# Linear attention followed by a gelu MLP, one core: pair layout of k and v in two batches, x inside the first h tiles, v casts moved, q transposed by DMA

## The chip, the cores and the metric

The kernel runs on one core of one Trainium2 chip. The metric is device time in microseconds (us); lower is better. The kernel before takes 309.27 us (median of 3 runs, 308.99 to 309.62). A profile gives the "span", from the first to the last instruction, which lies 1.8 to 2.1 us under the time of the same run. Engines are named as in the profile: PE (TensorE matmul), DVE (VectorE), ACT (ScalarE), POOL (GpSimd), SP (SyncE, here the queue that issues nearly all DMA transfers).

## The reference, cut to what matters

Inputs: q, k, v of 8 batches x 8 heads x 576 rows x 64 columns; w_in 512 x 2048; w_out 2048 x 512; all float32.

```python
q_s = softmax(q, axis=-1)            # over the 64 columns
k_s = softmax(k, axis=2)             # over the 576 rows
kv  = einsum('bhsd,bhse->bhde', k_s, v)
x   = einsum('bhsd,bhde->bhse', q_s, kv)   # then heads side by side: 4608 x 512
h   = x @ w_in                       # 4608 x 2048
out = gelu_erf(h) @ w_out            # 4608 x 512
```

The 4608 rows go through in nine chunks of 512: rows 0 to 511 of each batch (chunks 0 to 7) and the last 64 rows of all batches together (chunk 8).

## The kernel before

Per chunk there is an h phase (16 tiles of 4 matmuls, each tile followed by a gelu on ACT) and a y phase (4 accumulators of 16 matmuls, each followed by an eviction on DVE and a store). The attention of a later batch is put between these matmuls by hand; every engine works its instructions off in program order. A pair is two of the eight heads (pairs 0 to 3); kv and x are made by pairs. w_in and w_out are loaded in parts, w_in in five (0 to 4), w_out in four (0 to 3). The parts of the code that matter here:

```python
def norm_q(b, parts=1, engs=None):        # e = exp(q)
    ...                                   # per part:
        nc.vector.reduce_sum(out=qsum[:, :, hs], in_=eq[:, :, hs, :], axis=AX.X)
        nc.vector.reciprocal(recq[:, :, hs], qsum[:, :, hs])
        engs[i % len(engs)].tensor_tensor(out=eq..., in0=eq..., in1=recq..., op=ALU.mult)

def tp_step(b, half, eng="v"):            # q to columns, on PE
    ps = psum_a.tile([128, J, 2, 128], BF16, tag="a")
    ...                                   # 8 x nc.tensor.transpose(ps, eq, identity)
    nc.vector.tensor_copy(out=o, in_=ps)  # or ACT

def dve_front(b):
    norm_q(b)                             # the product on GpSimd
    if b < B:
        cast_v_all(b)                     # 5 casts on VectorE

# ... loads of batch 0, w_in, w_out, batch 1, batch 2 ...
kv_chain(0, warm)                         # casts, kv, norm, x of batch 0, one after the other
h_phase(0, {...})
y_phase(0, {(2, 0): [norm_q(1)], (3, 3): [tp_step(1, 0)], (3, 7): [tp_step(1, 1, "s")]})
kv_chain(1)                               # the same for batch 1, after y phase 0
h_phase(1, {12: [cast_v_all(2)]})
y_phase(1, {(0, 15): [norm_q(2)], (1, 15): [kv_step(2, ...)], ...})
for c in range(2, B + 1):
    # h phase c: kv of batch c+1 after tiles 1, 2; tp_step after 4, 5; x after 8..11
    # y phase c: (1, 15): dve_front(c + 2)
```

(Lambdas and repeated arguments are cut.) A main load has runs of 1024 B and, for the last 64 rows, a second transfer with runs of 256 B.

The softmax here doesn't subtract the row's maximum and nothing guards it: scores larger than these inputs give would overflow.

## Time and profile before

| | before |
|---|---|
| time, us | 309.27 |
| span of the profiled run, us | 307.6 |
| PE busy | 288.6 us, 94% |
| mean granted clock of PE | 0.972 |
| DMA, mean rate | 151 GB/s |

How to read it: PE is busy nearly throughout, so the question for each part is whether it takes work out of PE's full stretch or closes one of its holes, all of which lie before 95 us. A phase of 64 undisturbed matmuls is 13.81 us. The lines are shown in the prediction.

### The profile page before, as it was taken

To read this page: it belongs to the slowest core of one execution; us is meant where nothing else is said; L and a number is where in the kernel's file an instruction comes from. 1 tells how busy PE (TensorE), PEld (TensorE's weight loads), DVE (VectorE), ACT (ScalarE), POOL (GpSimd) and SP (SyncE) were. 2 spreads that over 40 slices of the span, in tenths; PEclk is the share of its full clock that TensorE was granted. 3 is DMA by queue.
4 is the path that set the end of the run, shared out by engine and by line. 5 is a ranking of instruction groups with operands and counts; after the bars stand their busy time and mean duration, and the time that the engine had idled before them with its cause. 6 is when DMAs were issued, how large, how long until landed. Compare 5 with 4: busy or idle time off the path is not lost.

```text
span 307.6 us, 3824 instructions
## 1 busy us (share of the span) xinstructions
PE 288.6 (94%) x1541; PEld 138.4 (45%) x1541; DVE 122.0 (40%) x218; ACT 151.7 (49%) x212; POOL 38.3 (12%) x23
## 2 busy tenths in 40 slices
PE   5759998699899999999999999999999999999993
PEld 1424444244445544544454445444644455444441
DVE  4754437410777355342534344434433223110021
ACT  4546754367924582458245924591457056006400
POOL 6200002000204206000600060006000400000000
PEclk9588999699999999999999999999999999999999
DMA  7999999995026902691279117911600100110033
GB/s 219 316 381 387 369 263 304 312 304 152 2 102 190 286 23 84 188 271 51 73 207 270 37 69 213 265 36 68 153 21 34 70 34 0 36 70 33 2 68 68
DMA packets 47809, 46.38 MB, mean 151 GB/s; under 512 B 14000, under 2 KB 39600, under 8 KB 47792
## 3 DMA queue, kind: packets, MB, share of 16 engines
q1 hardware_dynamic: 47792, 46.14, 51.4%
q8 instruction: 12, 0.20, 0.3%
q14 instruction: 5, 0.04, 0.0%
HBM read 36.70 MB, written 9.44 MB: 150 GB/s over the span
## 4 chain that ended last, share of the span: by engine, by line
PE 89%; DVE 4%; ACT 3%; DMA 2%; issue 1%; POOL 1%; SPq 0%; ACTq 0%; DVEq 0%
PE ps L246 42%; PE ps L259 38%; PE ps L209 3%; PE ps L169 3%; PE ps L225 2%; DMA f<-in_q_dram 2%; ACT e L123 1%; DVE qsum L159 1%; PE ps L328 1%; DVE y_sb L266 1%; POOL e L161 1%; DVE xT L235 1%; PE ps L173 1%; DVE kvbd L197 0%; ACT L123 0%
## 5 line engine op out<-in xcount | busy, mean ns | idle before, releaser
L250 ACT ACTIVATE g<-ps 128x512 bf16<-128x512 f32 x144 | 86.0, 597 | 116.1 <-PE ps L246 116.1
L246 PE MATMUL ps<-xT,wi_bf 128*128 128x512 bf16 x576 | 136.5, 386 | 1.7 <-ACT wi_bf L294 1.7
L259 PE MATMUL ps<-wo_bf,g 128*128 128x512 bf16 x576 | 126.6, 379 | 1.2 <-DVE y_sb L266 1.2
L259 PEld LDWEIGHTS <-g 128*128 128x128 bf16 x576 | 56.3, 98 | 68.8 <-issue 1.9
L246 PEld LDWEIGHTS <-wi_bf 128*128 128x128 bf16 x576 | 55.9, 99 | 66.2 <-issue 4.7
L266 DVE COPY y_sb<-ps 128x512 f32<-128x512 f32 x36 | 24.8, 689 | 96.9 <-PE ps L259 96.9
L161 POOL TENSOR_TENSOR e<-e,recq 128x2048 bf16<-128x2048 bf16 (+1 forms) x9 | 33.9, 3765 | 203.8 <-DVE recq L160 171.4
L123 ACT ACTIVATE e<-f 128x2048 bf16<-128x2048 f32 (+1 forms) x20 | 31.2, 1563 | 7.9 <-DMA f<-in_q_dram 4.3
L235 DVE CAST xT<-ps 128x512 bf16<-128x512 f32 x32 | 21.8, 689 | 20.1 <-PE ps L225 16.8
L159 DVE TENSOR_REDUCE qsum<-e 128x16 f32<-128x1024 bf16 (+1 forms) x12 | 20.9, 1743 | 19.1 <-ACT e L123 18.9
L216 DVE COPY qT<-ps 128x1024 bf16<-128x1024 bf16 x17 | 11.6, 690 | 15.3 <-PE ps L209 15.3
L169 PE MATMUL ps<-v_aug,e 128*128 128x129 bf16 x128 | 11.7, 228 | 4.6 <-DVE v_aug L144 2.8
L209 PE MATMUL ps<-identity,e 128*128 128x128 bf16 x144 | 11.7, 229 | 4.0 <-POOL e L161 3.9
L169 PEld LDWEIGHTS <-e 128*128 128x128 bf16 x128 | 9.5, 101 | 9.9 <-DVE v_aug L144 2.6
L209 PEld LDWEIGHTS <-e 128*128 128x128 bf16 x144 | 9.9, 102 | 8.5 <-POOL e L161 5.0
L225 PE MATMUL ps<-qT,kvbd 128*128 128x512 bf16 x32 | 12.2, 401 | 1.5 <-ACT kvbd L193 1.2
L144 DVE CAST v_aug<-f 128x512 bf16<-128x512 f32 x32 | 11.7, 415 | 2.5 <-DMA f<-in_v_dram 2.5
L79 ACT ACT_TABLE_LOAD x9 | 11.5, 1283 | 0.9 <-PEq L439 0.7
L328 PE MATMUL ps<-zeros 128*128 128x512 bf16 x21 | 7.9, 528 | 1.2 <-DVE scr L69 1.2
L186 DVE RECIPROCAL rec<-ps 128x2 f32<-128x2 f32 (+1 forms) x18 | 3.0, 169 | 14.6 <-PE ps L173 14.6
L197 DVE TENSOR_TENSOR kvbd<-ps,rec 64x128 bf16<-64x128 f32 (+1 forms) x30 | 8.4, 278 | 0.9
L123 ACT ACT_TABLE_LOAD x6 | 7.7, 1283 | 0.1
(32 smaller groups left out, 63.1 us busy)
## 6 DMA issues: line engine op xcount, KB each, us to landing
out_dram<-y_sb SPq DMA_DIRECT2D x32, 256.0 KB, 2.3
f<-in_q_dram SPq DMA_DIRECT2D x6, 1024.0 KB, 7.5
f<-in_k_dram SPq DMA_DIRECT2D x6, 1024.0 KB, 10.5
f<-in_v_dram SPq DMA_DIRECT2D x6, 1024.0 KB, 10.2
w<-in_moe_w_out_dram SPq DMA_DIRECT2D x4, 1024.0 KB, 11.4
w<-in_moe_w_in_dram SPq DMA_DIRECT2D x3, 1024.0 KB, 11.1
f<-in_q_dram SPq DMA_DIRECT2D x4, 512.0 KB, 9.2
f<-in_k_dram SPq DMA_DIRECT2D x4, 512.0 KB, 8.9
```

The lines of the kernel that those rows point to most:

```text
L123: nc.scalar.activation(out=dst[:, i * n:(i + 1) * n], in_=src[:, i * n:(i + 1) * n], func=AF.Exp)
L144: nc.vector.tensor_copy(out=o[:, :, :, 0:D], in_=s[:, hp])
L159: nc.vector.reduce_sum(out=qsum[:, :, hs], in_=eq[:, :, hs, :], axis=AX.X)
L161: engs[i % len(engs)].tensor_tensor(out=eq[:, :, hs, :], in0=eq[:, :, hs, :], in1=recq[:, :, hs].unsqueeze(3).to_broadcast([128, J, n, D]) ...
L169: nc.tensor.matmul(ps, st[b]["ek"][:, j, hs, :].rearrange("p h d -> p (h d)"), v_aug[b % 2][:, j, hp, 0:PW], start=(j == 0), stop=False,)
L209: nc.tensor.transpose(ps[:, j, i, :], st[b]["eq"][:, j, 2 * hp:2 * hp + 2, :].rearrange("p h d -> p (h d)"), identity,)
L225: nc.tensor.matmul(ps, kvbd[b][:, hp, :], st[b]["qT"][:, :, hp, :], start=True, stop=True)
L235: nc.vector.tensor_copy(out=st[b]["xT"][:, hp, :], in_=ps)
L246: nc.tensor.matmul(ps, wi_bf[:, dm, t * 128:(t + 1) * 128], xT[:, dm, :], start=(dm == 0), stop=(dm == NDM - 1),)
L250: nc.scalar.activation(out=g[:, t, :], in_=ps, func=AF.Gelu)
L259: nc.tensor.matmul(ps, g[:, t, j * 128:(j + 1) * 128], wo_bf[:, t, :], start=(t == 0), stop=(t == NDF - 1),)
L266: nc.vector.tensor_copy(out=y_sb, in_=ps)
```

## The change

Its intent, in four parts. (1) k and v of batches 0 and 1 are loaded with 9 consecutive rows of one head on a partition: one run of 9 x 64 x 4 = 2304 B, one transfer where there were two; kv is then made by 9 matmuls per pair of heads. (2) x pairs 2 and 3 of batches 0 and 1 are made inside the first group of h tiles, and y phase 0 runs over four accumulators at once so that batch 1's attention lies between its matmuls. (3) q of batches 3 to 8 is transposed by DMA and not by PE. (4) The v casts of batches 4 to 7 no longer follow the norm of q. Besides: GpSimd casts some of v and w_in, 30 warming matmuls instead of 12, the last store in halves.

```diff
+    def load_pair(b, name, t, parts):
+        src = t[b].rearrange("h (p n) d -> (h p) (n d)", n=NS).rearrange("(x q) f -> q x f", q=128)
+        ...
+    def kv_pair(b, hp):
+        for n in range(NS):                       # NS = 9
+            nc.tensor.matmul(ps[:, 0:D + 1], ek_pair[...][:, hp % 2, n, :], v_pair[b][:, hp, n, 0:D + 1], ...)
+    def xbar_step(b):
+        nc.sync.dma_start_transpose(out=qT as (p, 16, 128), in_=eq as (p, 2048))
...
-    kv_chain(0, warm)
+    kv_pair(0, 0) ... norm_pair(0, 3, "s")
+    cast_wi(2, wi[2], "v")
+    h_phase(0, {...}, group=3, pre={1: [x_step(0, 2)], 2: [x_step(0, 3, "s")]})
...
-    y_phase(0, {...})
-    kv_chain(1)
+    for t in range(12):
+        for j in range(J): y_mm(0, yps[j], j, t)
+        if t == 9: tp_step(1, 0)
+    # then t = 12..15 of one accumulator after the other, with tp, kv and x of batch 1 between
...
     y_phase(1, {
-        (0, 15): [norm_q(2, parts=2)],
+        (0, 15): [norm_q(2, 0, 2)],
+        (1, 1): [norm_q(2, 1, 2, nc.vector)],
...
-    s[4 + d] = [lambda: tp_step(b, 0)]
-    s[5 + d] = [lambda: tp_step(b, 1)]
...
-            yi[(1, 15)] = [lambda nb=nb: dve_front(nb)]
+            yi[(1, 0)] = [lambda nb=nb: norm_q(nb)]
+            if nb == 4:
+                yi[(2, 0)] = [lambda: cast_v_all(4)]
+            elif nb < B:
+                yi[(0, 8)] = [lambda nb=nb: cast_v_all(nb)]
+            yi[(3, 0)] = [lambda nb=nb: xbar_step(nb)]
```

## The prediction

> **What bounds the kernel now.** I read the page of the profile first (engine shares, 40 slices), then the chain that ended last in order of time, then the timeline of the first 95 us, then the windows. The page says that TensorE (PE) carries the end:
>
> ```profile
> PE 288.6 (94%) x1541; PEld 138.4 (45%) x1541; DVE 122.0 (40%) x218; ACT 151.7 (49%) x212; POOL 38.3 (12%) x23
> PE   5759998699899999999999999999999999999993
> PEclk9588999699999999999999999999999999999999
> DMA  7999999995026902691279117911600100110033
> PE 89%; DVE 4%; ACT 3%; DMA 2%; issue 1%; POOL 1%; SPq 0%; ACTq 0%; DVEq 0%
> L209 PE MATMUL ps<-identity,e 128*128 128x128 bf16 x144 | 11.7, 229 | 4.0 <-POOL e L161 3.9
> ```
>
> PE is full from slice 8 on, at full clock; holes and half clock stand in slices 0 to 3 and 7, where the DMA engines are saturated. So time can come from two places only: the head (to about 95 us) and PE work taken out of the full stretch. The chain shows where (start us, us, what):
>
> ```profile
> 21.24 15.67 PE ps L246 x64
> 36.91 11.22 PE ps L259 x52
> ...
> 51.76 0.69 DVE y_sb L266
> ...
> 59.15 15.49 PE ps L246 x64
> ...
> 76.58 1.92 ACT e L123
> ...
> 102.07 0.45 PE ps L209 x8
> ...
> 103.38 0.45 PE ps L209 x8
> ...
> 275.20 13.81 PE ps L246 x64
> ...
> 302.87 0.69 DVE y_sb L266
> ```
>
> A dense 64-matmul phase costs 13.81 us (216 ns each) when nothing disturbs it. From this I made a ledger of the span: start to the first h matmul 21.2; 18 dense phases 18 x 13.81 = 248.7; h phases 0 and 1 over that, 15.67 - 13.81 = 1.9 and 15.49 - 13.81 = 1.7; transposes in y phase 0, 1.0; the hole between y phase 0 and h phase 1, 59.15 - 51.76 = 7.4; y phase 1 (74.5 to 93.1) over 13.81, 4.8; five batches 3 to 7 with 2.9 of attention on PE each (16.7 - 13.8 for the h phase in the windows), 14.5; batch 8, 1.8; tail after the last matmul 4.7. Sum 307.7, the span being 307.6. The time is 1.7 above the span (309.27 - 307.6).
>
> **What the Trainium skill says.** "TensorE: Matmul & The Clock Gate", Part 1 (What's actually happening): the array falls to half clock after an idle window of about 3.4 us and needs as long a busy one to come back. The trace agrees: after PE idled from 5.5 to 9.4 us the windows show a granted clock of 0.50 for 8 to 14 us, and again 0.50 at 22 to 24 and 56 to 62 us, where matmuls start 428 ns apart, not 216. "SBUF — State Buffer", Who interferes with whom: a VectorE cast in a two-port mode and a GpSimd instruction exclude one another. The trace agrees: GpSimd's 128x2048 product takes 4.91 us beside the v casts and 3.6 in batch 8, which has none. "GPSIMD Engine Reference", introduction: elementwise work runs about twice as fast on VectorE; no GpSimd cast is in this trace. "DMA: Bandwidth & Descriptors", Latency and other measured facts: a DMA transpose moves 261 GB/s where the middle dimension isn't contiguous, so 512 KB would be 2 us of transfer, an estimate; no run shows one yet.
>
> **Part 1: transposes by DMA, batches 3 to 8.** Removed from PE: 6 batches x 2 halves x 0.45 us (the chain's L209 x8 pieces) = 5.4 us, all on the path, since PE is full there. Removed from VectorE: 12 evictions of 0.69 us, hidden anyway. Added: six transposes in the sync queue. In a steady y phase starting at T, exp of q ends at T+3.7, the reduction runs after the first y eviction (T+4.4 to 6.7), GpSimd's product ends at about T+11, and the queue reaches the transpose after the third output, about T+11.3. It's needed by the first x matmul, after h tile 8, T+22.7. Slack 11 us, against a landing I estimate at 4 to 6 us (2 of transfer, 2.3 to landing as the small outputs show, some issue). Hidden. Batch 3 is tighter: both product halves end about 5.6 us into h phase 2, x comes after tile 12 (12.3 us): 6.7 us of slack. I allow 0.5 for it. The v casts move away from the product; that shortens it to 3.6, not on the path.
>
> **Part 2: batch 0.** k and v (2.36 MB) moved at a mean of 289 GB/s (window 6 to 13 us), with dips to 164 to 230 where the 256 B rests were in flight; weights with longer runs got 382 (24 to 37 us). At 375 it takes 6.3 us and not 8.2: everything behind comes 1.9 us earlier. The third w_in part, cast at 20.5 before, lands near 18.6. Exps of k cost more: four of 64x1152 at about 1.16 (scaled from 1.06 for 1024 columns) for 2.75 before; they end near 12.6. The kv pairs are 9 matmuls of 65 columns at about 57 ns (the 129-column ones start that far apart), 0.5 each. GpSimd casts three v quarters and four w_in halves; at an estimated 0.7 us each it ends at 16.8. So the first group of three h tiles can begin near 16, but in VectorE's order the eviction of x pair 2 stands behind the cast of w_in part 2: it comes near 20, and the group's last six matmuls after it. Six earlier ones (1.3 us) are already done: an effective start of 18.8, plus 0.4 for two x inside: 19.2 for 21.2. PE idles some 3 us before it, so I keep 1.7 for half clock.
>
> **Part 3: batch 1 inside y phase 0.** The phase runs t-outer over four accumulators up to t = 11, so transposes, kv and x sit between matmuls. The 7.4 us hole and the 1.7 at half clock go. In their place: transposes 0.9, four kv pairs 2.0, four x 0.9, and 0.5 of the last kv to x chain not covered: 4.3 for 1.0 + 7.4 + 1.7 = 10.1. The loads allow it: h phase 0 ends near 34, w_out part 3 lands near 37 and is cast by ScalarE about 40, needed at 45; k and v of batch 1 land near 41 and 44, kv starts at 47.
>
> **Part 4: y phase 1.** In the old order both reductions and the product of q stood ahead of the first y eviction, which came at 83.1, 6 us after its accumulator was done. Now only the first half stands ahead of it: eviction about 5.4 us into the phase, the buffer needed at 6.9. Left over: 2.9 of attention and about 0.7 waiting for exp of k: 3.6 for 4.8.
>
> **Part 5: the end.** The last eviction and store in halves on two queues: 4.2 for 4.7.
>
> **Sum.** 19.2 + 248.7 + 1.7 + 4.3 + 3.6 + 5 x 2.0 + 0.9 + 0.5 + 4.2 = 293.1 of span; plus 1.7 is 294.8. By part: head 2.2, batch 1 5.8, y phase 1 1.2, transposes 5.4 less 0.5, tail 0.5. I place the centre at 293.0, somewhat lower, since the 30 warming matmuls may save the half clock that I keep in h phase 0.
>
> **Rivals.** (a) The DMA transpose is slow, or holds up the sync queue. Nothing in the old trace measures it. Against it: 11 us of slack, and the 40-slice DMA row shows stretches of 0 to 2 tenths in each y phase. If landing took 15 us, x would wait about 4 us in each of six batches and in batch 3 more: 24 us back, a little above where it began at 310 to 320, the only way to slower. (b) The head stays bound by loads: the w_in parts set when h tiles can go (casts at 20.5, 23.2, 25.9 waited for the DMA), so reordering attention gives only 1.9 us, and in-order queues (GpSimd casts at twice my estimate, the eviction behind the cast) give that back: 297 to 299. (c) The gain of batch 1 is given back in y phase 1: it starts some 9 us earlier while batches 2 and 3 still load (the old trace's loads ended at 74 us). If they end about 70, exp of batch 3 has little margin; a late one delays h phase 2's gelus by 1 to 3 us. (d) PE stays warm throughout and the first group starts near 17: about 289.
>
> **Range and chances.** Parts 1 and 3 (some 11 us) rest on counted PE work and a visible hole; the head is uncertain by 3 each way. I predict 293.0, range 287.5 to 298.5. Faster by over 2% means under 303.1: it takes both rival (a) and another to miss it. Faster 0.95, within 2% 0.03, slower 0.02.
>
> **What would show it.** L209's successors: 48 PE transposes, not 144, and h phases of 15.8 us in batches 3 to 7, not 16.7, with no wait of x for the transpose; its landing under 10 us. First dense h stretch from about 20 and h phase 0 ending near 34. Full clock from 46 us on; h phase 1 beginning near 51 and ending near 66, not 74.5. The first y eviction of y phase 1 about 5.4 us in. Wrong would be: x waiting for the transpose each batch, half clock at h phase 1, loads of batch 3 ahead of an exp in the chain.

## The result, and the profile after

The changed kernel takes 294.3 us (median of 4 runs, 292.78 to 295.34) beside 309.36 for the kernel before (the three runs above and a fourth). The ratio is 0.951, 95% interval 0.9459 to 0.9562. Ratios here are the mean time of one kernel's fast runs over that of the other's of the same rounds, so not quite the ratio of the medians.

The page of the kernel after, the rows that answer to those shown of before (engines; PE, clock and DMA in 40 slices; the chain by engine):

```profile
PE 279.7 (96%) x1491; PEld 132.1 (45%) x1491; DVE 118.8 (41%) x211; ACT 154.8 (53%) x212; POOL 38.6 (13%) x34
PE   8849999999999999999999999999999999999993
PEclk9999999999999999999999999999999999999999
DMA  7999999999118946981698079816601600120033
PE 81%; DMA 9%; SPq 3%; DVE 2%; ACT 2%; issue 1%; ACTq 0%
```

PE has 9 us less of work and no hole after slice 2 that a tenth would show; the clock row is full in this run (although the first warming matmuls, until about 5 us, still start 0.43 us apart, not 0.216: the row doesn't show that cold start). The chain that ended last now goes through DMA for 9% of the span: 16.6 us in the head, which hangs on loads, and 10.0 us for the v of batch 5. In order of time (start us, us, what):

```profile
8.23 10.21 DMA w<-in_moe_w_in_dram
...
18.47 1.23 DVE wi_bf L403
19.70 0.61 DVE xT L318
...
20.35 1.04 PE ps L336 x4
...
33.44 8.63 PE ps L346 x40
...
97.58 13.81 PE ps L346 x64
...
132.30 0.44 DVE v_aug L210
...
134.12 0.61 DVE y_sb L365
...
134.77 7.07 PE ps L346 x32
```

(L336 are the h matmuls, L346 the y matmuls.) The first three lines are one story: a load of w_in, VectorE's cast of it, and only then the eviction of x that PE waits for until 20.35. The last three are another: a v cast, a y eviction behind it, and PE going on at 134.77. Cutting both chains at the same phase starts gives a ledger of the spans:

| stretch | before, us | after, us | less, us |
|---|---|---|---|
| start to y phase 0 | 36.91 | 33.44 | 3.47 |
| y phase 0, batch 1's attention, h phase 1 | 37.76 | 31.39 | 6.37 |
| y phase 1 | 18.49 | 16.94 | 1.55 |
| h and y phase 2 | 30.52 | 29.62 | 0.90 |
| h and y phase 3 | 30.52 | 30.45 | 0.07 |
| h and y phases 4 to 6 | 91.55 | 88.87 | 2.68 |
| h and y phase 7 | 29.45 | 28.56 | 0.89 |
| phase 8 and tail | 32.40 | 32.13 | 0.27 |
| sum | 307.60 | 291.40 | 16.20 |

Phases 2 to 7 would each give 0.9 by the DMA transposes; five of them do, and phase 3 gives nearly none. (In what was expected of the runs below, "batch 4" is this phase 3: batch 4's kv and x are made in it.) The trace by the tile that the transposes write, of the kernel after (issuing queue, instruction, count: ns min/median/max; then from issue to landing):

```profile
L289 SPq DMA_TRANSPOSE qT<-e x6: 1372/2078/2280, 87.4 to 228.5; - x6
DMA to landing us min/median/max: 4.3/4.4/4.9
```

The transpose issued at 111.41 landed 4.6 us later, near 116.0; x of that batch began after kv and nine tiles, at 120.1. No instruction waits for one.

The four runs of the changed kernel fall in two groups: 292.78 and 293.42 with a mean clock of 0.997 and 1.000, 295.18 and 295.34 with 0.991 and 0.988. Experiments e6 and e9 look into that.

### The profile page after: what moved, and what is told of

Same layout as the page of the kernel before. It is cut to its first block, busy times and chain, and to the rows that moved or that the text cites. A ratio compares the mean times of both kernels' runs of the same rounds, so it can differ in the third digit from the quotient of the medians.

```text
span 291.4 us, 3728 instructions
## 1 busy us (share of the span) xinstructions
PE 279.7 (96%) x1491; PEld 132.1 (45%) x1491; DVE 118.8 (41%) x211; ACT 154.8 (53%) x212; POOL 38.6 (13%) x34
## 4 chain that ended last, share of the span: by engine, by line
PE 81%; DMA 9%; SPq 3%; DVE 2%; ACT 2%; issue 1%; ACTq 0%
PE ps L346 38%; PE ps L336 38%; DMA w<-in_moe_w_in_dram 4%; DMA f<-in_v_dram 3%; DMA f<-in_k_dram 2%; SPq L121 2%; PE ps L237 2%; PE ps L305 2%; ACT ek L152 1%; PE ps L272 1%; DVE v_aug L210 1%; SPq L105 0%; DVE xT L318 0%; ACT L152 0%; PE ps L241 0%
## 5 line engine op out<-in xcount | busy, mean ns | idle before, releaser
L336 PE MATMUL ps<-xT,wi_bf 128*128 128x512 bf16 x576 | 132.3, 379 | 4.1 <-DVE xT L318 2.4
L346 PE MATMUL ps<-wo_bf,g 128*128 128x512 bf16 x576 | 127.9, 379 | 0.7 <-DVE y_sb L365 0.7
L336 PEld LDWEIGHTS <-wi_bf 128*128 128x128 bf16 x576 | 55.4, 98 | 69.3 <-issue 3.9
L346 PEld LDWEIGHTS <-g 128*128 128x128 bf16 x576 | 56.0, 98 | 67.0 <-issue 0.9
L229 POOL TENSOR_TENSOR e<-e,recq 128x1024 bf16<-128x1024 bf16 (+1 forms) x10 | 27.6, 2761 | 184.2 <-DVE recq L228 145.1
L152 ACT ACTIVATE e<-f 128x1024 bf16<-128x1024 f32 (+1 forms) x11 | 15.7, 1442 | 2.9 <-DMA f<-in_q_dram 2.8
L210 DVE CAST v_aug<-f 128x512 bf16<-128x512 f32 x24 | 10.3, 428 | 10.2 <-DMA f<-in_v_dram 9.5
L152 ACT ACTIVATE ek<-f 128x2048 bf16<-128x2048 f32 x6 | 11.4, 1898 | 0.0
L424 PE MATMUL ps<-kvbd 128*128 128x512 bf16 x35 | 9.7, 440 | 1.2 <-DVE scr L82 1.2
L202 DVE CAST vr_aug<-f 64x512 bf16<-64x512 f32 x6 | 5.6, 926 | 11.7 <-DMA f<-in_v_dram 11.7
L168 ACT ACTIVATE ek<-f 64x1152 bf16<-64x1152 f32 x8 | 9.3, 1162 | 1.3 <-DMA f<-in_k_dram 1.1
L237 PEld LDWEIGHTS <-ek 128*128 128x128 bf16 x96 | 6.8, 97 | 3.2 <-ACT ek L152 0.6
L237 PE MATMUL ps<-v_aug,ek 128*128 128x129 bf16 x96 | 8.1, 220 | 0.1
L259 DVE TENSOR_TENSOR kvbd<-ps,rec 64x128 bf16<-64x128 f32 x24 | 6.9, 289 | 0.6
```

The lines of the kernel that those rows point to most:

```text
L152: nc.scalar.activation(out=dst[:, i * n:(i + 1) * n], in_=src[:, i * n:(i + 1) * n], func=AF.Exp)
L210: nc.vector.tensor_copy(out=o[:, :, :, 0:D], in_=s[:, hp])
L229: eng.tensor_tensor(out=eq[:, :, hs, :], in0=eq[:, :, hs, :], in1=recq.unsqueeze(3).to_broadcast([128, J, w, D]), op=ALU.mult,)
L237: nc.tensor.matmul(ps, st[b]["ek"][:, j, hs, :].rearrange("p h d -> p (h d)"), v_aug[b % 2][:, j, hp, 0:PW], start=(j == 0), stop=False,)
L336: nc.tensor.matmul(ps, wi_bf[:, dm, t * 128:(t + 1) * 128], xT[:, dm, :], start=(dm == 0), stop=(dm == NDM - 1),)
L346: nc.tensor.matmul(ps, st[c]["g"][:, t, j * 128:(j + 1) * 128], wo_bf[:, t, :], start=(t == 0), stop=(t == NDF - 1),)
```

## The experiments

All are edits of the changed kernel, all gave correct results. Runs e1 to e4 shared one chip, e5, e6, e7 and e9 another, and e8, e10, e11 and e12 a third; medians and ratios are of their 4 to 6 runs, spans of the profiled one, to be read against 291.4. The changed kernel was not run again beside them, and its own runs spread over 2.6 us, so a difference of a few tenths between spans is read from the phases of the traces and not from the times.

**e1: the transposes back on PE.**

```diff
+        s[10 if late else 4] = [lambda: tp_step(b, 0)]
+        s[11 if late else 5] = [lambda: tp_step(b, 1)]
-        xbar_step(3)
-            yi[(3, 0)] = [lambda nb=nb: xbar_step(nb)]
```

> The changed kernel with the transposes of q of batches 3 to 8 put back on TensorE (h tiles 4 and 5, batch 3 at 10 and 11) and the DMA transposes gone. Theory (transposes on TensorE are pure added length where it is full, 0.90 us a batch): span 291.4 + 6 x 0.9 = 296.8, h phases of 16.7 us instead of 15.8. Part of the 0.85 us lost in batch 4 may come back, since the queue no longer carries the transposes: 296 to 297. Rival (the gain of batches 3 to 8 came from VectorE's or GpSimd's relief): no change from 291.4.

298.24 us, ratio 0.9651, span 296.2. Each pair of phases from 2 to 6 takes 30.52 us, 16.71 of it the h phase, as in the kernel before. Phase 3 loses only 0.07 by it, the five others 0.9 each; with 0.3 of a later start that is 4.9, and 4.8 was measured. So the DMA transposes are worth 0.9 us wherever PE is full. Phase 3's missing 0.8 is not a separate matter: the transpose stands in the one sync queue ahead of the loads of batch 5. That queue's timeline, of the kernel after first, then of e1:

```profile
111.41 2.27 SPq L289 DMA_TRANSPOSE qT<-e  x1
...
122.33 1.19 SPq L122 DMA_DIRECT2D f<-in_v_dram  x1
```

```profile
119.33 1.64 SPq L122 DMA_DIRECT2D f<-in_v_dram  x1
```

Counted from the start of h phase 3 (111.2 and 112.4), the v of batch 5 is issued at 11.1 us with the DMA transposes and at 6.9 without, and its casts begin at 21.1 and at 17.4 (20.0 to 20.7 in e4, e5, e6, e11 and e12, which keep the DMA transposes and these casts). In e1 PE waits for no y eviction, so the 0.8 comes back, as its expectation had allowed.

**e3: the v casts back behind the norm of q.**

```diff
             yi[(1, 0)] = [lambda nb=nb: norm_q(nb)]
-            if nb == 4: yi[(2, 0)] = [cast_v_all(4)]
-            elif nb < B: yi[(0, 8)] = [cast_v_all(nb)]
+            if nb < B: yi[(1, 0)].append(cast_v_all(nb))
```

> The changed kernel with the v casts of batches 4 to 7 put back right after the reduction of q, beside GpSimd's product. Theory (keeping them apart isn't worth anything by itself; it costs 0.7 us once, where the early cast of batch 5 waits for its v and holds up a y eviction): GpSimd's 128x2048 products 4.9 us instead of 3.6, span 0.5 to 0.9 us shorter, about 290.7. Rival (the casts kept apart are what lets the DMA transposes hide): x waits for the transposes, span longer by 1 us or more.

309.13 us, ratio 1.0008, span 307.9: the whole gain of the change is gone, and both expectations are wrong. x doesn't wait for a transpose, and the product isn't stretched to 4.9. VectorE's timeline in y phase 3 of this run (start us, us, engine, line, what):

```profile
138.08 0.35 DVE L228 RECIPROCAL recq<-qsum 128x32 f32<-128x32 f32 x1
138.35 0.36 DVE L202 CAST vr_aug<-f 64x512 bf16<-64x512 f32 x1
138.63 5.10 DVE L210 CAST v_aug<-f 128x512 bf16<-128x512 f32 x4
143.64 1.28 DVE L365 COPY y_sb<-ps 128x512 f32<-128x512 f32 x2
```

Four casts that take 0.43 each elsewhere take 5.10 together: the chain of this run shows one of them at 3.74, nearly the length of GpSimd's product, which ran from 138.56 for 3.95 us. The y eviction stands behind them, and PE's timeline of the same run has the price:

```profile
137.64 4.26 PE L346 MATMUL ps<-wo_bf,g 128*128 128x512 bf16 x18
144.37 5.30 PE L346 MATMUL ps<-wo_bf,g 128*128 128x512 bf16 x16 [2.47 <-DVE y_sb L365]
```

PE waits 2.47 us, and the 16 matmuls after it take 5.30 us; after the same wait in phase 2, of 2.71 us, they took 3.61. The windows show a granted clock of 0.61 and 0.53 from 144 to 148 us, and of 1.00 after the wait in phase 2. Against the changed kernel, phases 2 to 5 of this run are 2.9, 3.5, 4.4 and 4.3 us longer, 15.1 together (the four waits are 10.2 us, and half clock after three of them about 1.7 each); y phase 0 began 1.5 later, with half clock in the head. That is the 16.5 by which the spans differ.

In the kernel before, the casts stand beside the product too, and it is the product that gives way. Its timeline around the same place (from two engines, in order of time):

```profile
96.52 0.36 DVE L136 CAST vr_aug<-r 64x512 bf16<-64x512 f32 x1
...
96.77 4.91 POOL L161 TENSOR_TENSOR e<-e,recq 128x2048 bf16<-128x2048 bf16 x1 [14.68 <-PE ps L246]
96.80 1.41 DVE L144 CAST v_aug<-f 128x512 bf16<-128x512 f32 x4
```

There VectorE was first with its casts back to back and the product ended 1.3 us late, which nobody waited for; in e3 the product got in between two casts. The program gives both kernels the same order (reduction, product, casts); why VectorE kept its turn in the one and not in the other isn't shown.

**e9: the v casts all beside the product, but behind the second y eviction.**

```diff
-            if nb == 4: yi[(2, 0)] = [cast_v_all(4)]
-            elif nb < B: yi[(0, 8)] = [cast_v_all(nb)]
+            if nb < B: yi[(2, 0)] = [cast_v_all(nb)]
```

> The changed kernel with the v casts of batches 4 to 7 all at the place that batch 4 has: beside GpSimd's product, but behind the second y eviction. The run with the casts ahead of that eviction took 15 us more. Theory (what costs is not the overlap of cast and product but a y eviction that stands behind the blocked cast): one cast of each batch still takes about 3.5 us, no wait of TensorE for a y eviction, each batch 29.6, span 290.5 to 291.5. Rival (the overlap itself costs, wherever it stands): span 300 or more.

293.54 us, ratio 0.9496, span 291.9. The casts of the 64 leftover rows in this run (count: ns min/median/max):

```profile
L202 DVE CAST vr_aug<-f x6: 399/3367/3472, 54.6 to 195.4; 64x512 bf16<-64x512 f32 x6
```

The median is 3367 ns, so they are blocked as in e3, and no y eviction holds PE up: all pairs of phases take 29.6. So what cost 15 us in e3 wasn't the overlap but what stood behind it in VectorE's queue. "Kept apart" is one way out, a harmless place is another.

This run's profile is also of the slower kind (clock 0.991). Its windows (stretch, us, busy us of PE, its loads, DVE, ACT, POOL; clock; DMA share; GB/s):

```profile
18.00:20.00 2.00, 0.17 (x1) 0.00 (x0) 1.29 (x2) 0.59 (x1) 0.00 (x0) 1.00 1.04 380
20.00:22.00 2.00, 1.41 (x4) 0.56 (x4) 0.71 (x2) 0.00 (x0) 0.00 (x0) 0.58 1.04 387
22.00:24.00 2.00, 2.00 (x7) 0.67 (x5) 1.05 (x1) 1.51 (x3) 0.00 (x0) 0.57 1.05 387
```

After PE's idle time before 20.6 us the clock is at 0.58 and 0.57: in 4 us it loses about 4 x 0.42 = 1.7 us. In the profiled run of the changed kernel the same windows read 1.00.

**e7: the v casts of batches 4 and 5 behind the third y eviction.**

```diff
-            if nb == 4: yi[(2, 0)] = [cast_v_all(4)]
+            if nb in (4, 5): yi[(3, 0)] = [cast_v_all(nb)]
```

> The changed kernel with the v casts of batches 4 and 5 moved behind the third y eviction of the phase (batch 4 from ahead of it, batch 5 from ahead of the first). Theory (batch 4 costs 30.45 us instead of 29.62 because the casts of batch 5, put ahead of the first y eviction, wait for their v until 132.3 us, and TensorE then 0.66 us for that eviction): batch 4 takes 29.6, span 0.8 us shorter, 290.6. Rival (batch 4 waits for something else, such as a transpose): 30.4 stays.

293.23 us, ratio 0.9492, span 291.0; phase 3 takes 29.6 and PE waits for no y eviction. The trace agrees with the theory, but the time doesn't prove it: e11 and e12 leave these casts where the change has them, and there too phase 3 takes 29.6 (29.75 in e5, 30.0 in e6). The place is on the edge: in the changed kernel the eviction, 0.68 us long, began 7.0 us after the y phase began, and PE wanted the accumulator at 7.07; in e5 it began at 6.3. Whether that wait comes depends on how soon the v of batch 5 lands, which the transposes ahead of it put off (e1).

**e5: VectorE's cast of w_in part 2 behind the eviction of x pair 2.**

```diff
-    cast_wi(2, wi[2], "v")
     h_phase(0, {
...
-        1: [lambda: x_step(0, 2)],
+        1: [lambda: x_step(0, 2), lambda: cast_wi(2, wi[2], "v")],
```

> The changed kernel with VectorE's cast of w_in part 2 moved behind the eviction of x pair 2 of batch 0 (in program order; nothing else changes). Theory (TensorE waits from 17.97 to 20.35 us only because that eviction stands behind a cast that waits for its load until 18.47): the eviction comes near 17.1, the first three h tiles end near 19, the next wait is tile 4 for w_in part 2 near 19.7; y phase 0 begins near 30.8 instead of 33.4 and the span is 2.0 to 2.7 us shorter, 288.7 to 289.4. Rival (the loads set the head): later h tiles wait for w_in parts 3 and 4 or y phase 1 for loads of batches 2 and 3, and under 0.7 us of it arrives.

290.88 us (290.43 to 292.35), ratio 0.9418, span 288.8, 2.6 under 291.4. PE's timeline of this run:

```profile
18.43 1.56 PE L336 MATMUL ps<-xT,wi_bf 128*128 128x512 bf16 x6
20.24 11.38 PE L336 MATMUL ps<-xT,wi_bf 128*128 128x512 bf16 x51 [0.25 <-ACT g L341]
31.46 8.80 PE L346 MATMUL ps<-wo_bf,g 128*128 128x512 bf16 x39
```

The last six matmuls of the first group start at 18.43, not 20.35, although the same load landed 0.6 us later here (its cast began at 19.04, not 18.47). No later phase gave the gain back. But only 1.8 of the 2.6 us arose in the head (y phase 0 began 1.8 us earlier, less than the 2.6 expected); the other 0.7 is phase 3, 29.75 for 30.45, where this run's v happened to land in time. e8 has the same edit with the load as early as in the changed kernel (cast at 18.47), and there the head gains 2.35.

**e6: matmuls on zeros in PE's idle time.**

```diff
-        2: [lambda: x_step(0, 3, "s")],
+        2: [lambda: x_step(0, 3, "s"), lambda: warm_a(12)],   # 12 matmuls of 128x512 on zeros
```

> The changed kernel with 12 more matmuls on zeros (2.6 us at full clock) in TensorE's idle time between 17.9 and 20.3 us. Theory (the runs of the changed kernel at 293 and at 295 us, with mean clocks of 1.00 and 0.99, differ by half clock after that idle time): all runs near 293 with mean clock 0.997 or more, the spread of 2.6 us gone. Rival (the runs differ by something else): times spread from 292.8 to 295.4 as before.

293.46 us, ratio 0.9499; five runs from 292.93 to 294.58, all with a clock of 0.997 or more. The half-clock kind is gone in five of five, as the theory said (of the four runs of the changed kernel two had it). Five runs are few: e1, e7, e9 and e12, which have the same head, were under 0.995 in 6 of 16. And the spread doesn't vanish: 1.65 us remain at full clock, and the median gained little. A second source shows in the traces: the cast of w_in part 2, which waits for nothing but its load, begins between 18.47 and 19.74 us in the profiled runs of the kernels that leave the head's loads alone (19.74 in e6), so the first loads alone vary by over a microsecond from run to run and chip to chip. How much of that is the chip can't be told from one profile of each. A third source is the warming itself: the 30 warming matmuls take 8.27 to 9.50 us in the profiled runs and end after the half product that the first transposes need (9.2 us), so they put off batch 0's first transposes by up to 1.3 us. Whether 30 are better than 12 was not tested.

**e8: both mends, e5 and e7.** The edit is the two diffs together.

> The changed kernel with both mends: the cast of w_in part 2 behind the eviction of x pair 2, and the v casts of batches 4 and 5 behind the third y eviction. Theory (the two savings are apart in time, 2.6 and 0.8 us, and add up unless the earlier start already removed the second): span 288.0 to 288.8, time 289.7 to 290.8, no run with a clock under 0.997. Rival (the second saving is not there any more once the head is shorter, since that run showed no wait for a y eviction): no better than the 290.9 of the first alone.

290.4 us (290.2 to 292.35, 6 runs), ratio 0.9414, span 288.2. Against the changed kernel's 0.951 that is 1% less, by intervals that don't overlap, from different rounds; e5 alone has nearly the same ratio (0.9418). Of the 3.2 us of span 2.35 are the head and 0.8 phase 3; e7's part adds nothing that the times can show. Two runs of six had a clock just under the 0.997 that I had named (0.996 and 0.994, the latter with the 292.35 us).

**e2 and e10: the loads of k and v of batches 0 and 1 in three pieces.** In e2 by columns (runs of 1024, 1024 and 256 B), in e10 by partitions (runs of 2304 B):

```diff
 # e2
+            for lo, hi in ((0, 256), (256, 512), (512, 576)):
+                nc.sync.dma_start(out=f[:, i*n:(i+1)*n, lo:hi], in_=src[:, i*n:(i+1)*n, lo:hi])
 # e10
+            for lo, hi in ((0, 48), (48, 96), (96, 128)):
+                nc.sync.dma_start(out=f[lo:hi, i*n:(i+1)*n, :], in_=src[lo:hi, i*n:(i+1)*n, :])
```

> The changed kernel, same tiles and arithmetic, but each k and v load of batches 0 and 1 cut into three transfers with runs of 1024, 1024 and 256 B. Theory (long runs bring all later loads 1.9 us earlier and h phase 0 hangs on w_in part 2): w_in part 2 is cast 1 to 2 us later than 18.47, span 1 to 2 us longer, about 293. Rival (the head hangs on the order of VectorE and GpSimd, not on loads): landing later but span within 0.3 us of 291.4.

> The changed kernel with each k and v load of batches 0 and 1 cut into three transfers by partitions (48, 48 and 32), so as many transfers as in the run with short runs, but with runs of 2304 B. Theory (the short runs themselves made that run 5 us slower): near 291.4 span, w_in part 2 cast within 1 us of 18.5. Rival (the number of transfers did it, by their issue in the one queue): w_in part 2 cast near 22 and span near 296.

e2: 297.94 us, ratio 0.9608, span 296.5, w_in part 2 cast at 22.13. e10: 299.4 us, ratio 0.9695, span 296.8, that cast at 23.43. e2 lost more than either of its expectations allowed. e10 went as its rival said: long runs in more transfers are no better than short ones. The windows from 10 to 14 us show where e2 lost, of the kernel after first, then of e2 (the last two numbers are DMA share and GB/s):

```profile
10.00:12.00 2.00, 1.64 (x20) 0.89 (x17) 1.36 (x3) 1.95 (x3) 1.79 (x2) 1.00 1.04 398
12.00:14.00 2.00, 1.33 (x28) 1.09 (x25) 1.81 (x7) 1.96 (x3) 1.34 (x2) 1.00 1.09 355
```

```profile
10.00:12.00 2.00, 1.64 (x17) 0.89 (x15) 1.35 (x2) 1.95 (x3) 1.45 (x2) 1.00 0.94 257
12.00:14.00 2.00, 1.68 (x36) 1.39 (x35) 1.45 (x6) 1.59 (x3) 0.99 (x2) 1.00 0.71 174
```

In e2 the DMA engines run dry (share 0.71): the issue of w_in began at 12.18 us and not at 4.79. The issue times fit a limit of eight transfers under way (in e2 the ninth was issued at 4.90), which was not tested by itself. In the changed kernel exactly eight transfers stand ahead of w_in, and its issue begins at 4.79 us, just after the first q had landed (ACT's exp of it began at 4.61). e10 is no clean control, though: its engines were busy (share 1.0) at 207 to 241 GB/s from 6 to 16 us, so its transfers were slow for another reason than too few under way, presumably the split by partitions. How much of the head's gain is due to run length and how much to fewer transfers stays open.

**e4: y phase 0 in the old order, batch 1's attention after it.** The t-outer loops are replaced by:

```diff
+    y_phase(0, {(0, 15): [norm_q(1, 0, 2)], (1, 15): [norm_q(1, 1, 2, nc.vector), v casts on GpSimd],
+                (3, 3): [tp_step(1, 0)], (3, 7): [tp_step(1, 1)]})
+    kv_pair(1, 0) ... norm_pair(1, 3, "s")
```

> The changed kernel with y phase 0 in the old order (one accumulator after the other) and kv and x of batch 1 after it; x pairs 2 and 3 still inside the first h tiles. Theory (the interleaving closes the hole between y phase 0 and h phase 1): a hole of 3 to 5 us comes back, and half clock with it in h phase 1 where it is long enough: span 294 to 297. Rival (the hole was closed by earlier loads and the pair layout alone): span within 0.7 us of 291.4.

301.56 us, ratio 0.9753, span 300.0: 8.6 more, above the expected range. PE's timeline of the run names a second wait that I hadn't counted:

```profile
40.57 11.75 PE L346 MATMUL ps<-wo_bf,g 128*128 128x512 bf16 x39 [3.64 <-ACT wo_bf L417]
```

The change loads w_out part 3 behind q of batch 1 and casts it on ACT; in the old order the thirteenth y matmul already needs it, in the new one the 49th. So the interleaving hides 3.64 us of a late load; of the 8.5 us that y phase 0 to h phase 1 take longer, the other 4.9 are put down to the attention hole, by difference. The half clock that was expected with it didn't come (1.00 in all windows from 52 to 66 us).

**e11: x pairs 2 and 3 before the first h tile.** The `group` and `pre` arguments are removed and the two x_step calls of each batch put ahead of h_phase.

> The changed kernel with x pairs 2 and 3 of batches 0 and 1 made before the first h tile, as in the kernel before, and no grouping of h tiles. Theory (the early matmuls of the group fill TensorE's wait for the late pairs: six in batch 0, four in batch 1): 1.3 us later in batch 0 and 0.9 in batch 1, span 293 to 294, or 295.5 with half clock. Rival (they only move work about): within 0.5 us of 291.4.

296.49 us, ratio 0.9604, span 294.3. In the head 2 h matmuls ran before the wait and not 6, 0.9 us; from y phase 0 to the end of h phase 1 it took 0.4 us more. The rest of the 2.9 is this run's later load (cast at 19.66, 1.2 later) and half clock in the head, less the 0.8 of phase 3. So this part is worth about 1.3 us directly, somewhat less than expected, and keeps PE's idle time short: three of its four runs had a clock of 0.988.

**e12: both halves of batch 2's norm ahead of the first y eviction of y phase 1.**

```diff
-        (0, 15): [norm_q(2, 0, 2)],
-        (1, 1): [norm_q(2, 1, 2, nc.vector)],
+        (0, 15): [norm_q(2, 0, 2), norm_q(2, 1, 2, nc.vector)],
```

> The changed kernel with both halves of q's norm of batch 2 ahead of the first y eviction of y phase 1, as in the kernel before. Theory (that order held the accumulator and made TensorE wait): the first eviction moves from 69.3 to 72.5 us and TensorE waits 0.3 to 0.8 us for it, span 291.7 to 292.3. Rival (the gain in y phase 1 comes from x spread over the last accumulator alone): no wait for a y eviction, span 291.4.

294.83 us, ratio 0.9543, span 293.0. The eviction came at 74.11, 7.6 us into the phase, PE waited 0.6 us for it, and the phase took 17.7 us, not 16.9. In the trace that is as expected; the span of 293.0 is above the expected 292.3, because the head ended 1.7 us later (a later load and half clock) and phase 3 was 0.8 shorter. The time alone doesn't show the effect: the interval of the ratio, 0.9515 to 0.957, overlaps the changed kernel's.

Not tested apart: the 30 warming matmuls, the casts on GpSimd, x of batch 2 spread over the last accumulator, and the last store in halves.

## Why the prediction was right, point by point

The time of 294.3 lies within the range of 287.5 to 298.5, 1.3 above the centre; by the ledger each term was met to within 1.3 us. The working's own sum, 294.8, was nearer than the centre of 293.0 that was placed below it in the hope of full clock: two of the four runs had it. The range holds both kinds of run; how many of four are of which kind is luck. The ledger is of a full-clock run (293.42). (18 x 13.81 is 248.6, not the 248.7 of the working.)

- **The transposes (part 1).** 0.9 us a batch, on the path, and hidden in their place: right, by the ledger and by e1. The landing estimated at 4 to 6 us was 4.3 to 4.9. The Trainium skill's figure in "DMA: Bandwidth & Descriptors", Latency and other measured facts (261 GB/s, by estimate 2 us for 512 KB), was used for the transfer only; landing took over twice that.
- **What failed there.** The sum had 0.5 for batch 3, which lost nothing, and nothing for phase 3, which lost 0.8. The step "the v casts move away from the product; that shortens it to 3.6, not on the path" had the right 3.6 but missed both ways in which those casts reach the path: ahead of the first y eviction they wait for a load that the transpose in the same queue puts off (0.66 us of PE, once), and behind the earlier norm they would have been blocked ahead of an eviction (e3, 15 us).
- **The head (part 2).** 2.2 us expected with 1.7 of half clock kept; 3.5 measured at full clock, and 2.1 in e9's run at half clock. The eviction behind the cast came where it was put (19.6 for "near 20"), w_in part 2 at 18.47 for 18.6, GpSimd's end at 17.0 for 16.8 (0.67 us for a v quarter, 0.59 for a w_in half). That this order is the cause is shown by e5 and e8. The reason for the earlier load is only half right: 375 GB/s was assumed for long runs, and the four windows from 6 to 14 us read 332, 400, 398 and 355, but e2 and e10 don't let run length be held apart from the number of transfers.
- **Batch 1 (part 3).** 5.8 expected, 6.4 measured. e4 shows that the interleaving does it, 4.9 us of hole, and that it hides a late w_out part as well.
- **y phase 1 (part 4).** 1.2 expected, 1.55 measured; the eviction came 4.5 us into the phase and not 5.4. e12 shows 0.6 to 0.8 of it as the norm's order. The prediction's "6 us after its accumulator was done" is a misreading: the sixteenth y matmul ended near 78.1 and the eviction came at 83.1, 5 us.
- **The end (part 5).** 0.5 expected, 0.27 measured for phase 8 and the tail.
- **The rivals.** A slow transpose (a) didn't occur, but its second half, that it holds up the sync queue, did in small: the v of batch 5 about 4 us later, 0.8 us of one phase (e1). (b), loads and in-order queues, describes what is left in the head; e5 took 1.8 us of it back and e8 2.35. (c), loads of batches 2 and 3 late for y phase 1, didn't occur. (d), PE warm throughout, was true of half the runs, yet with the first group not near 17 it gave 293 and not 289; e5 and e8 show the 290 that lies there.
- **The clock.** The working says that the trace agrees with an idle window of about 3.4 us. That holds for its first case (idle from 5.5 to 9.4 us). The other two followed shorter idle times: at most 1.75 us before the half clock at 22 to 24 us, and 1.45 before that at 56 to 62.

## What to carry to other kernels

Moving work off a full engine is worth what it takes there, if its replacement's landing time fits the slack; read both from the trace and it can be counted in advance. Where one engine serves both evictions and side work in program order, ask of each side instruction what it may wait for, a load or another engine's lock, and put it behind the eviction that the full engine needs next: here that was worth about 2 us once, and 15 us where it was got wrong. A transfer that replaces work of an engine also takes a place in its queue: look at what is issued behind it. When loads bound the start, count transfers as well as bytes: cut into three, the same loads cost 4 to 5 us, with short runs and with long ones (e2, e10).

## What the Trainium skill lacked or had wrong

- "SBUF — State Buffer", Who interferes with whom: that whoever issues first has the ports and the other is blocked fits what the runs show. It lacks what this means for a row of casts: in the kernel before the product began before four of the five casts and still ended 1.3 us late (4.91 for 3.62), as if VectorE had kept its turn over the whole row; in e3 and e9 one cast took 3.4 to 3.7 us instead of 0.4, and what was queued behind it came later.
- "TensorE: Matmul & The Clock Gate", Part 1: it names an idle window of about 3.4 us. Here 2.42 us of idle time (e9) and 2.47 and 2.54 (e3) were enough for half clock, while 2.41 (the profiled run of the changed kernel) and 2.71 (e3, phase 2) weren't. What decides between them isn't shown.
- "DMA: Bandwidth & Descriptors", DMA Transpose (X-bar): no time for one transpose between SBUF addresses. 128 x 2048 bf16 took 4.3 to 4.9 us from issue to landing, and held its queue for 1.4 to 2.3 us; a load issued behind it in the same queue came about 4 us later.
- "GPSIMD Engine Reference", introduction: "roughly 2×" for VectorE. A float32 to bf16 cast of 128 x 576 took 0.67 us on GpSimd; VectorE takes 0.42 for 128 x 512, so 1.4 times by the element; for w_in it was 0.59 for 128 x 512 against VectorE's 1.23 for 128 x 2048, 1.9 times for the same number of elements.
